# Fillers on a tile of ones at the head, weight sums over both tiles of a pair, strided probabilities turned by VectorE alone

## The chip, the cores and the metric

The kernel runs on one core of one Trainium2 chip. Its engines work side by side and meet at semaphores: TensorE (PE in the profile, its weight loads PEld), VectorE (DVE), ScalarE (ACT), GpSimd (POOL) and SyncE (SP), which here only issues transfers. The metric is the device time of one execution in microseconds, the median of several runs. In a matmul row, `ph<-xc,wi 128*128 128x512` means that the product goes to the tile ph, from a stationary 128x128 block and 512 moving columns.

## The reference, cut to what matters

Attention over 8 batches of 8 heads, 576 positions of 64 numbers, with two masks, and then a feed-forward layer on 4608 tokens:

```python
scores = scale * np.matmul(q, k.transpose(0, 1, 3, 2))
rel = pos[:, None] - pos[None, :]
mask_local = (rel >= 0) & (rel < 32)                                       # heads 0 to 3
mask_strided = (rel >= 0) & (pos[None, :] % 32 == pos[:, None] % 32)       # heads 4 to 7
attn = np.exp(scores - max); attn = attn / (sum + 1e-09)
x = np.matmul(attn, v)                  # -> [4608, 512]
h = x @ w_in                            # 512 -> 2048
g = h * np.clip(h + 3.0, 0.0, 6.0) / 6.0
return g @ w_out                        # 2048 -> 512
```

q, k and v are float32; w_in and w_out come as 64-bit floats and are turned into pairs of reduced-precision parts on the chip.

## The kernel before

**Order.** The kernel doesn't issue its work as it is written. Each piece of work (an "op") is given to a planner (class `Plan`) with the engine or engines that may do it, an estimated duration, what it reads and writes, and a due time. `Plan.emit` then plays the work through with those durations, always taking the op that can begin first (the earlier due time breaks ties), and writes one fixed order for each engine. On the chip each engine works through its list in that order and waits where a semaphore tells it to. Due times are built on the constant `T0`, the time at which the first feed-forward tile is planned to begin.

**Fillers.** Where the planner sees TensorE idle before 100 us (`WARM`), it puts fillers in: matmuls of 128x512 whose result nobody reads (function `idle`, L1625). `LIT` is the time from which TensorE can begin, `COLD` the time until which the planner counts TensorE's work 1.8 times as long and spaces fillers by `IDLE` (0.43) and not `HOT` (0.22). Before `COLD` it puts at least two fillers in front of each op. The fillers multiply `eye`, a bfloat16 identity made by GpSimd (L256 and L257), by itself. No filler is written once the second `ph` bank exists.

**The head.** Batch 0's attention comes first, in four pairs of heads. q and k are loaded in rows and turned by TensorE (L536), scores are made with the mask added by a matmul with eye (strided heads L689 and L693, local heads L659 to L670), brought to SBUF (L683 to L706), and normalized: maximum on VectorE (L724, L727), difference on GpSimd (L731, L746), exponential on ScalarE (L734, L749), sum and inverse on VectorE (L738 to L757), product on GpSimd (L742, L761). For strided heads the probabilities are then turned in blocks of 32x32 and laid on the diagonal of a cleared tile, for which the products with v (L879) need them. In batch 0 this is done in two steps: `turn` (L810), one transpose by VectorE into the kept tile `atk`, and `spread` (L817 or L819), two ops of two copies each, on ScalarE or GpSimd as the planner finds best. In later batches VectorE transposes four quarters straight into place (L807), except in batch 1, which reads `atk` as it is. In the same time the weights come in as 64-bit numbers, pass through two ScalarE steps (L340, L344), a join on VectorE (L348), a rounded high part (L356 on ScalarE, L358 on GpSimd) and a low part (L366). The first feed-forward tile (`ffn(0)`, products L1040 to L1042 and L973 to L975) begins when x and the first weights are there.

**Pairs of tiles.** Tiles 3 to 8 are done in three pairs (`PAIRS`, `ffn_pair`), with seven products in place of eight for the first layer. A pair has a first half, eight steps m of seven products into two banks `ph` (L1214 to L1216), evacuated to htmp (L1225, L1227, L1233) and gated (L1075, L1079), with the second layer of the pair's first tile in between; and a second half, 16 chunks fc of twelve products (L973 to L975) for its second tile, whose g is split into a high part (ScalarE, L1006) and a low part (GpSimd, L1009). Output weights come from DRAM into a ring of four buffers (`second_weights`, L948).

**Sums of weights.** The third pair needs sums and differences of output weights. They are made during the second pair by `combine_out(m, ...)`, once for each m from 0 to 7, out of the two weight tiles 2m and 2m+1 that are in the ring at that time: two whole sums (L1302), four differences of halves (L1306), two roundings on ScalarE (L1310), two remainders (L1313), and six stores to DRAM on SP's queue (L1318, L1321). All work in one set of four buffers, `("xf", 1, c)`, named hxf in the profile, so a sum can begin only when the stores of the sum before have been read out. The third pair loads them back (L1411).

Of the kernel before, what the change touches and what calls it, by code (L numbers as in the profile page):

```python
# [20 lines left out]
P = 128  # L21
# [8 lines left out]
PAD = 32  # L30
# [12 lines left out]

T0 = 42.0
TILE = 98.5
SOLO = 3
ADDED = 3
# [16 lines left out]
HOT = 0.22  # L66
FETCH = 2.2
BEGIN = 0.75
LIT = 1.7
LAND = 4.6  # L70
COLD = 8.6
WORDS = 256
AHEAD_OF = 63
REFILL = 3.2
# [6 lines left out]
class Plan:  # L81
# [29 lines left out]
    def emit(self, idle):  # L111
        ops = self.ops
        nexts = [[] for _ in ops]
        left = [len(o[2]) for o in ops]
        for n, o in enumerate(ops):
            for m in o[2]:
                nexts[m].append(n)
        ready = {e: [] for o in ops for e in o[0]}
        free = {e: LIT if e == "PE" else BEGIN for e in ready}
        avail = [o[9] for o in ops]  # L120
        slots = {}
        mode, dma, port = "", LAND, 0.0
        held, turned = AHEAD_OF, 0.0

        def admit(n):
            for e in ops[n][0]:
                heapq.heappush(ready[e], (ops[n][3], n))

        for n, k in enumerate(left):
            if k == 0:  # L130
                admit(n)
        order = []
        done = 0
        while done < len(ops):
            done += 1
            best = None
            for e, r in ready.items():
                t0, first, kept = free[e], None, 0.0
                for due, n in sorted(r):
                    t = max(t0, avail[n] + (PATIENCE.get((e, ops[n][11]), 0.0) if WARM < avail[n] < CALM and len(ops[n][0]) > 1 else 0.0))  # L140
                    if ops[n][11] and e in PORT:
                        t = max(t, port)
                    take = ops[n][7]
                    if take is not None:
                        many = take if isinstance(take, list) else [take]
                        s = max(kept, sorted(slots.get(k, 0.0) for k in many[0].among)[len(many) - 1])
                        if s > t and t <= t0:
                            kept = s
                        t = max(t, s)
                    if first is None or (t, due, n) < first:  # L150
                        first = (t, due, n)
                if first is not None and (best is None or first[:2] < best[3]):
                    best = (first[0], e, first[2], first[:2])
            t, e, n, _ = best
            how, fn, _, due, _, m, after, take, give, _, words, shared = ops[n]
            for x in how:
                ready[x].remove((due, n))
            for x in take if isinstance(take, list) else [take] if take else []:
                x.key = min(x.among, key=lambda k: (slots.get(k, 0.0) > t, x.among.index(k)))
                slots[x.key] = float("inf")  # L160
            if e == "PE" and t < WARM:
                one = IDLE if free[e] < COLD else HOT
                many = max(int((t - free[e]) / one), 2 if t < COLD else 0)
                t = max(t, free[e] + many * one)
                for i in range(many):
                    order.append((free[e] + i * one, len(order), None, e))
                    held += 2
            start = t
            if e == "PE" and m != mode:
                t += 0.09  # L170
                mode = m
            self.by[n] = e
            us = how[e]
            free[e] = end = t + (us() if callable(us) else us) * (1.8 if e == "PE" and t < COLD else 1.0)
            if shared and e in PORT:
                port = end - 0.13
            if e == "PE":
                held += words
                while held >= WORDS:
                    held -= WORDS  # L180
                    free[e] = end = turned = max(end, turned + (SLOWER if turned < 40.0 else REFILL))
            if after:
                end = dma = max(t + FETCH, dma) + after
            if give is not None:
                slots[give.key] = end + HOP
            order.append((start, len(order), n, e))
            for k in nexts[n]:
                hop = HOP if e not in ops[k][0] or after else 0.02
                avail[k] = max(avail[k], end + hop + ops[k][4])
                left[k] -= 1  # L190
                if left[k] == 0:
                    admit(k)
        for _, _, n, e in sorted(order):
            if n is None:
                idle()
            elif len(ops[n][0]) > 1:
                ops[n][1](e)
            else:
                ops[n][1]()
# [9 lines left out]
def attention_ffn(ctx: ExitStack, tc, q, k, v, w_in, w_out, out):  # L209
# [33 lines left out]


    three = const.tile([P, 1], F32, name="three")
    eye = const.tile([P, P], BF16, name="eye")
    mband = const.tile([QB, 2 * PAD], BF16, name="mband")
    mfirst = const.tile([PAD, PAD], BF16, name="mfirst")
# [3 lines left out]
    left = [const.tile([P, B * LEFT], F32, name=f"left{c}") for c in range(NCC)]  # L252

    def identity():
        nc.vector.memset(three, 3.0)
        make_identity(nc, new(const, ("ident",), [P, P], F32, "ident"))  # L256
        nc.gpsimd.tensor_copy(eye, tiles["ident",])  # L257
# [215 lines left out]
    def kept_pair(g):  # L473
# [318 lines left out]
        def transposes(j):  # L792
            def tr():
                e = e_whole(j)
                if apart:
                    nc.vector.transpose(tiles["atk"][:, odd, j], e)
                    return
                at = tiles[akeys[j]]
                if loc:
                    for a in range(3):  # L800
                        for h in range(2):
                            nc.vector.transpose(at[PAD * (a + h):PAD * (a + h) + PAD, :, PAD * a:PAD * a + PAD],  # L802
                                                e[PAD * a:PAD * a + PAD, :, PAD * h:PAD * h + PAD])
                else:
                    for a in range(4):
                        rows = slice(PAD * a, PAD * a + PAD)
                        nc.vector.transpose(at[rows, :, rows], e[rows])  # L807

            def turn():
                nc.vector.transpose(tiles["atk"][:, odd, j], e_whole(j))  # L810

            def spread(e, h):
                for a in (2 * h, 2 * h + 1):
                    rows = slice(PAD * a, PAD * a + PAD)
                    to, what = tiles[akeys[j]][rows, :, rows], tiles["atk"][rows, odd, j]
                    if e == "ACT":
                        nc.scalar.copy(to, what)  # L817
                    else:
                        nc.gpsimd.tensor_copy(to, what)  # L819
            if early and not loc:  # L820
                op("DVE", 0.45, turn, reads=[ekey, ekey1, wkey("o", NQ - 1, 0)], writes=[("atk", odd, j)], due=due - 2 + j)
                for h in range(2):
                    op({"ACT": 0.84, "POOL": 0.7}, 0, partial(spread, h=h), reads=[("atk", odd, j), *([akeys[j]] if h else [])], writes=[akeys[j] + ("h",)] if h else [akeys[j]], due=due - 1.9 + j)
                return
            op("DVE", 6 * 0.37 if loc else 0.45 if apart else 4 * 0.435, tr, reads=[ekey, ekey1, *home], writes=[akeys[j]], due=due - 2 + j)

        if shifted:
# [46 lines left out]
        else:  # L874
# [26 lines left out]
                op("DVE", 0.16, fence, reads=vb, writes=[stkey], due=due - 1002)  # L901
                op("PE", 0.65 * slow, partial(half_mm, 1), reads=[*akeys, *home, vkey], writes=[*vb, *xk, lk], due=due - 1001, mode="v", words=130)
            else:
                op("PE", 1.3 * slow, both_mm, reads=[*akeys, vkey, *([x + ("h",) for x in akeys] if early else [])], writes=[*vb, *xk, lk], take=vb,
                   due=due - 1001, room=0.0 if early else ROOM, mode="v", words=64)
            puts = []
            for h in range(2):
# [264 lines left out]
    def ffn_pair(p, last=None):  # L1172
# [104 lines left out]
        for m in range(HALVES):  # L1277
            if m:
                wk = [second(2 * m - 2 + i, s0 + (m + 0.3 + 0.5 * i) * long) for i in range(2)]
                if p == len(PAIRS) - 2:  # L1280
                    combine_out(m - 1, s0 + (m + 1.0) * long, wk)
            pair_products(m)
        wk = [second(NFC - 2 + i, half - (0.4 - 0.2 * i) * long) for i in range(2)]
# [2 lines left out]
        for fc in range(NFC):  # L1286
# [1 line left out]
            gk = [("g", fc % 2, x) for x in range(2)]  # L1288
            split_g(fc, kept_g[fc], gk, at - 2000, names[1])
            when = [at + 0.2 * i * short for i in range(4)]  # L1290
            mm2(fc, gk, second_weights(fc, at), when.__getitem__, names[1], None, out_of(1, half + NFC * short))

    def combine_out(m, due, wk):

# [324 lines left out]
    def idle():  # L1619

        if ("ph", 1) in tiles:
            return
        if warm[0] is None:
            warm[0] = pp.tile([P, TOK], F32, tag="ph_1", name="idle")
        nc.tensor.matmul(warm[0].rearrange("p (u x) -> p u x", x=P), eye, eye.unsqueeze(1).to_broadcast([P, TOK // P, P]), start=True, stop=True)  # L1625

    with tc.manual_schedule():
        plan.emit(idle)
# [30 lines left out]
```

## Time and profile before

| | us |
|---|---|
| median of the runs | 896.52 |
| the runs | 892.78, 896.52, 1947.74 |
| the profiled execution | 905.56 |
| its span, first to last instruction | 903.7 |
| first product of the first feed-forward tile in that span | 50.30 |
| first half of the second pair | 527 to 699 |
| its second half | 699 to 743 |

The profiled execution is the one whose rows are quoted; it is slower than the two runs of ordinary length. Views used: the page; the timeline (start, duration, engine, line, operation, the tile written and those read, and in brackets the idle time before it and what ended it); the chain of work that ended last; the waits; stretches (busy time of PE, PEld, DVE, ACT and POOL, each with its count of instructions, then granted TensorE clock, DMA share and GB/s); and groups of one line (count: shortest, median and longest ns, first and last start). "Busy" is not the same as useful: fillers are busy too.

### The profile page before, as it was taken

Reading aid. Unit: us, or ns where it says so; the run is one execution under the profiler, and the core shown is the slowest. Engines: PE = TensorE matmul, PEld = TensorE weight load, DVE = VectorE, ACT = ScalarE, POOL = GpSimd, SP = SyncE. Lnnn points to the kernel's source line nnn. Section 1 sums busy time; section 2 is a strip of 40 time slices with the busy share of each in tenths; the row PEclk is TensorE's granted clock in tenths of the full one; section 3 lists DMA queues with packets and bytes.
Section 4 is the critical chain, followed back from the end, with each engine's and each line's share of the span. In section 5 each row is a group of like instructions: output and inputs, shape, how many; then the busy total and the mean of one; then the engine's idle time right before and its main releaser. Section 6 shows DMA issues by size and latency. Waiting matters only on the chain.

```text
span 903.7 us, 20479 instructions
## 1 busy us (share of the span) xinstructions
PE 885.3 (98%) x8048; PEld 724.7 (80%) x8048; DVE 585.9 (65%) x996; ACT 401.5 (44%) x717; POOL 476.3 (53%) x429
## 2 busy tenths in 40 slices
PE   9999999999998999999999999998999999999998
PEld 6777877878887888887878878887888888888898
DVE  3778776768875767786667843657658305656882
ACT  2686664343344334434334632443456223433730
POOL 4578777357766657422232944775679732231300
PEclk9999999999999999999999999999999999999999
DMA  8978798867988899998885598899777777555632
GB/s 187 295 183 179 200 309 241 202 175 201 230 197 248 253 219 210 277 233 206 217 201 179 161 299 210 276 259 277 239 256 237 243 233 250 188 199 183 187 132 69
DMA packets 233695, 197.54 MB, mean 219 GB/s; under 512 B 164608, under 2 KB 195328, under 8 KB 233600
## 3 DMA queue, kind: packets, MB, share of 16 engines
q1 hardware_dynamic: 233444, 195.94, 77.6%
q8 instruction: 64, 1.05, 0.6%
q10 hardware_dynamic: 156, 0.29, 0.1%
q14 instruction: 31, 0.25, 0.1%
HBM read 155.29 MB, written 40.89 MB: 217 GB/s over the span
## 4 chain that ended last, share of the span: by engine, by line
PE 88%; DVE 4%; DMA 3%; ACT 2%; POOL 1%; issue 1%; SPq 0%; DVEq 0%; ACTq 0%; POOLq 0%
PE ph L1214 8%; PE ph L1215 8%; PE ph L1216 8%; PE ph L1040 5%; PE acc L973 5%; PE ph L1042 4%; PE ph L1041 4%; PE acc L975 4%; PE acc L974 4%; PE ps L670 3%; PE az L1431 3%; PE az L1429 3%; PE az L1430 3%; PE pv L879 2%; PE pv L435 2%; PE acc1b L973 2%
## 5 line engine op out<-in xcount | busy, mean ns | idle before, releaser
L1214 PE MATMUL ph<-xc,wi 128*128 128x512 f32 x336 | 134.9, 401 | 4.3 <-DVE htmp L1233 2.6
L1215 PE MATMUL ph<-xc,wi 128*128 128x512 f32 x336 | 131.8, 392 | 0.0
L1216 PE MATMUL ph<-xc,wi 128*128 128x512 f32 x336 | 131.2, 391 | 0.0
L1233 DVE TENSOR_TENSOR htmp<-ph,htmp 128x512 f32<-128x512 f32 x72 | 49.5, 689 | 57.5 <-PE ph L1216 54.3
L1009 POOL TENSOR_TENSOR g<-u,g 128x512 fp32r<-128x512 f32 x48 | 63.9, 1333 | 40.4 <-ACT g L1006 26.8
L1214 PEld LDWEIGHTS ph<-xc,wi 128*128 128x128 f32 x336 | 63.3, 188 | 21.6 <-DVE htmp L1233 3.4
L973 PE MATMUL acc<-wo,g 128*128 128x512 f32 x192 | 77.8, 405 | 0.5 <-DMA wo<-wod 0.5
L975 PE MATMUL acc<-wo,g 128*128 128x512 f32 x192 | 75.8, 395 | 2.3 <-POOL g L1009 2.3
L1040 PE MATMUL ph<-x,wi 128*128 128x512 f32 x192 | 77.2, 402 | 0.3 <-POOL wi L358 0.3
L1042 PE MATMUL ph<-x,wi 128*128 128x512 f32 x192 | 75.2, 391 | 0.6 <-POOL wi L366 0.6
L974 PE MATMUL acc<-wo,g 128*128 128x512 f32 x192 | 75.3, 392 | 0.0
L1041 PE MATMUL ph<-x,wi 128*128 128x512 f32 x192 | 75.1, 391 | 0.0
L1216 PEld LDWEIGHTS ph<-xc,wi 128*128 128x128 f32 x336 | 63.4, 189 | 13.8
L1215 PEld LDWEIGHTS ph<-xc,wi 128*128 128x128 f32 x336 | 63.4, 189 | 10.9
L802 DVE STREAM_TRANSPOSE atloc<-e 32x192 f32<-32x192 f32 x168 | 61.9, 368 | 10.0 <-POOL e L761 6.2
L1075 ACT ACTIVATE u<-ph,three 128x512 f32<-128x512 f32 x48 | 33.1, 690 | 68.0 <-PE ph L1042 67.8
L746 POOL TENSOR_TENSOR e<-e,st 128x288 f32<-128x288 f32 (+1 forms) x30 | 34.1, 1137 | 39.6 <-DVE st L724 39.4
L1225 ACT COPY htmp<-ph 128x512 f32<-128x512 f32 x58 | 34.1, 587 | 46.1 <-PE ph L1216 43.9
L761 POOL TENSOR_TENSOR e<-e,st 128x288 f32<-128x288 f32 (+1 forms) x30 | 35.4, 1181 | 33.5 <-DVE st L757 28.7
L1079 DVE SCALAR_TENSOR_TENSOR u<-u,ph 128x512 f32<-128x512 f32 x48 | 33.0, 687 | 25.3 <-ACT u L1075 24.6
L1009 POOL TENSOR_TENSOR g10a<-u,g00a 128x512 fp32r<-128x512 f32 x16 | 21.4, 1336 | 50.4 <-ACT g00a L1006 41.8
L807 DVE STREAM_TRANSPOSE at<-e 32x256 f32<-32x256 f32 x96 | 41.7, 435 | 6.1 <-POOL e L761 4.9
(318 smaller groups left out, 2330.0 us busy)
## 6 DMA issues: line engine op xcount, KB each, us to landing
wo<-wod SPq DMA_DIRECT2D x96, 512.0 KB
wi<-wid SPq DMA_DIRECT2D x84, 512.0 KB
rawi<-in_moe_w_in_dram SPq DMA_DIRECT2D x16, 512.0 KB
rawo<-in_moe_w_out_dram SPq DMA_DIRECT2D x16, 512.0 KB
wod<-wo SPq DMA_DIRECT2D x16, 512.0 KB
wid<-st SPq DMA_DIRECT2D x64, 128.0 KB
qn<-in_q_dram SPq DMA_DIRECT2D x112, 72.0 KB
kn<-in_k_dram SPq DMA_DIRECT2D x112, 72.0 KB
```

Of the source, the lines that this page charges most:

```text
L802: nc.vector.transpose(at[PAD * (a + h):PAD * (a + h) + PAD, :, PAD * a:PAD * a + PAD], e[PAD * a:PAD * a + PAD, :, PAD * h:PAD * h + PAD])
L973: nc.tensor.matmul(acc, gh, woh, start=fc == 0, stop=False)
L974: nc.tensor.matmul(acc, gh, wol, start=False, stop=False)
L975: nc.tensor.matmul(acc, gl, woh, start=False, stop=end)
L1009: on(e).tensor_tensor(out=to(1), in0=tiles[uk], in1=tiles[gk[0]].bitcast(F32), op=ALU.subtract)
L1040: nc.tensor.matmul(ph, wih, xh, start=n_ == 0, stop=False)
L1041: nc.tensor.matmul(ph, wih, xl, start=False, stop=False)
L1042: nc.tensor.matmul(ph, wil, xh, start=False, stop=n_ == NCC - 1)
L1214: nc.tensor.matmul(ph, w[:, j, 0], x[:, 0], start=u in (0, 1, 3) and j == 0, stop=False, skip_group_check=u in (2, 4, 5, 6))
L1215: nc.tensor.matmul(ph, w[:, j, 0], x[:, 1], start=False, stop=False, skip_group_check=u in (2, 4, 5, 6))
L1216: nc.tensor.matmul(ph, w[:, j, 1], x[:, 0], start=False, stop=j == 1, skip_group_check=u in (2, 4, 5, 6))
L1233: nc.vector.tensor_tensor(out=tiles[s.key], in0=tiles[bank], in1=tiles[s.key], op=ALU.add)
```

## The change

It does four things. The fillers read a new tile `full`, all ones, written by VectorE's first instruction. The planner lets fillers begin at 1.1 and puts no other TensorE work before 7.0 (`RISEN`); it counts TensorE as slow until 7.0 in place of 8.6. `T0` goes from 42 to 40. In batch 0 the strided probabilities take the path of later batches (`tr`, L807), and `turn` and `spread` go, with the extra keys that the products with v waited for. In the second pair the sums for m = 1, 3, 5, 7 stay in the first half; those for m = 0, 2, 4, 6 are made in the second half, each after the chunk fc with fc % 4 == 1, out of the ring's tiles of chunks fc-1 and fc, which the second half loads anyway.

```diff
-T0 = 42.0
+T0 = 40.0
-LIT = 1.7
+LIT = 1.1
+RISEN = 7.0
-COLD = 8.6
+COLD = 7.0
...
+            if e == "PE":
+                t = max(t, RISEN)
             if e == "PE" and t < WARM:
                 one = IDLE if free[e] < COLD else HOT
                 many = max(int((t - free[e]) / one), 2 if t < COLD else 0)
...
+    full = const.tile([P, P], BF16, name="full")
...
     def identity():
+        nc.vector.memset(full, 1.0)
         nc.vector.memset(three, 3.0)
...
-            def turn():
-                nc.vector.transpose(tiles["atk"][:, odd, j], e_whole(j))
-
-            def spread(e, h):
-                for a in (2 * h, 2 * h + 1):
...
-            if early and not loc:
-                op("DVE", 0.45, turn, reads=[ekey, ekey1, wkey("o", NQ - 1, 0)], writes=[("atk", odd, j)], due=due - 2 + j)
-                for h in range(2):
-                    op({"ACT": 0.84, "POOL": 0.7}, 0, partial(spread, h=h), ...)
-                return
             op("DVE", 6 * 0.37 if loc else 0.45 if apart else 4 * 0.435, tr, reads=[ekey, ekey1, *home], writes=[akeys[j]], due=due - 2 + j)
...
-                op("PE", 1.3 * slow, both_mm, reads=[*akeys, vkey, *([x + ("h",) for x in akeys] if early else [])], ...
+                op("PE", 1.3 * slow, both_mm, reads=[*akeys, vkey], writes=[*vb, *xk, lk], take=vb,
...
-                if p == len(PAIRS) - 2:
+                if p == len(PAIRS) - 2 and m % 2 == 0:
                     combine_out(m - 1, s0 + (m + 1.0) * long, wk)
...
-            mm2(fc, gk, second_weights(fc, at), when.__getitem__, names[1], None, out_of(1, half + NFC * short))
+            wk = second_weights(fc, at)
+            held = [wk[0]] if fc % 2 == 0 else [*held, wk[0]]
+            mm2(fc, gk, wk, when.__getitem__, names[1], None, out_of(1, half + NFC * short))
+            if p == len(PAIRS) - 2 and fc % 4 == 1:
+                combine_out(fc // 2, at + 4 * short, held)
...
-        nc.tensor.matmul(warm[0].rearrange("p (u x) -> p u x", x=P), eye, eye.unsqueeze(1)...
+        nc.tensor.matmul(warm[0].rearrange("p (u x) -> p u x", x=P), full, full.unsqueeze(1)...
```

More of the change, by code (lines that the diff above doesn't have):

```diff
@@ L807, in tr @@
                         nc.vector.transpose(at[rows, :, rows], e[rows])
-            def turn():
-                nc.vector.transpose(tiles["atk"][:, odd, j], e_whole(j))
-            def spread(e, h):
-                for a in (2 * h, 2 * h + 1):
[L814 to L819, printed above, removed]
-            if early and not loc:
-                op("DVE", 0.45, turn, reads=[ekey, ekey1, wkey("o", NQ - 1, 0)], writes=[("atk", odd, j)], due=due - 2 + j)
-                for h in range(2):
-                    op({"ACT": 0.84, "POOL": 0.7}, 0, partial(spread, h=h), reads=[("atk", odd, j), *([akeys[j]] if h else [])], writes=[akeys[j] + ("h",)] if h else [akeys[j]], due=due - 1.9 + j)
-                return
             op("DVE", 6 * 0.37 if loc else 0.45 if apart else 4 * 0.435, tr, reads=[ekey, ekey1, *home], writes=[akeys[j]], due=due - 2 + j)
@@ L903, in kept_pair @@
             else:
-                op("PE", 1.3 * slow, both_mm, reads=[*akeys, vkey, *([x + ("h",) for x in akeys] if early else [])], writes=[*vb, *xk, lk], take=vb,
+                op("PE", 1.3 * slow, both_mm, reads=[*akeys, vkey], writes=[*vb, *xk, lk], take=vb,
                    due=due - 1001, room=0.0 if early else ROOM, mode="v", words=64)
@@ L1624, in idle @@
             warm[0] = pp.tile([P, TOK], F32, tag="ph_1", name="idle")
-        nc.tensor.matmul(warm[0].rearrange("p (u x) -> p u x", x=P), eye, eye.unsqueeze(1).to_broadcast([P, TOK // P, P]), start=True, stop=True)
+        nc.tensor.matmul(warm[0].rearrange("p (u x) -> p u x", x=P), full, full.unsqueeze(1).to_broadcast([P, TOK // P, P]), start=True, stop=True)
     with tc.manual_schedule():
```

## The prediction

> **What bounds the kernel now.** I read the page first (span, busy shares, chain), then the first 54 us of the timeline, where the change does most, then the chain from 42 to 54 us, then the second pair (527 to 743 us) by waits, stretches and groups. The fences hold chosen rows; rows between them are left out.
>
> ```profile
> span 903.7 us, 20479 instructions
> PE 885.3 (98%) x8048; PEld 724.7 (80%) x8048; DVE 585.9 (65%) x996; ACT 401.5 (44%) x717; POOL 476.3 (53%) x429
> PE 88%; DVE 4%; DMA 3%; ACT 2%; POOL 1%; issue 1%; SPq 0%; DVEq 0%; ACTq 0%; POOLq 0%
> ```
>
> TensorE is busy 98% of the span and is 88% of the chain that ended last. So a gain has to shorten what TensorE does, or close its gaps. Busy is not useful, though: the head holds fillers, and useful work at half speed.
>
> ```profile
> 0.81 0.06 DVE L255 MEMSET three<- 128x1 f32 x1 [0.81 <-PEq L1643]
> 1.71 4.45 PE L1625 MATMUL idle<-eye 128*128 128x512 bf16 x10 [1.71 <-POOL eye L257]
> 6.46 1.22 PE L536 MATMUL kp<-ident,kn 72*128 72x72 f32 x8 [0.30 <-DMA kn<-in_k_dram]
> 7.48 1.06 PE L1625 MATMUL idle<-eye 128*128 128x512 bf16 x2
> 13.75 1.99 PE L693 MATMUL ps<-kplain,qt 64*128 64x72 f32 x16
> 21.14 1.52 PE L670 MATMUL ps<-kplain,qplain 64*32 64x64 f32 x72
> 31.53 3.88 PE L1625 MATMUL idle<-eye 128*128 128x512 bf16 x10
> 34.49 0.15 PEld L1625 LDWEIGHTS <-eye 128*128 128x128 bf16 x1 [0.27 <-issue]
> 34.82 0.10 PEld L1625 LDWEIGHTS <-eye 128*128 128x128 bf16 x1 [0.17 <-issue]
> 35.25 0.49 PE L659 MATMUL ps<-mband,eye 96*96 96x384 bf16 x2
> 35.83 0.97 PE L670 MATMUL ps<-kplain,qplain 64*32 64x64 f32 x72
> 41.91 5.57 PE L1625 MATMUL idle<-eye 128*128 128x512 bf16 x25
> 53.70 0.50 PE L1040 MATMUL ph<-x,wi 128*128 128x512 f32 x1
> ```
>
> The same 72 matmuls of L670 take 1.52 us at 21 us and 0.97 us at 36 us. The first ten fillers come every 4.45/10 = 0.44 us, the 25 at 41.91 every 5.57/25 = 0.22 us. Between lies the third streak of fillers: it starts at 31.53 us, and the spacing of its weight loads falls below 0.43 us at 34.8. So in this execution TensorE ran at half rate until 34.8 us. The granted clock that the page gives there is full, so in the head the spacing has to be read, not that row. The first streak (1.71 to about 6.6 us, 4.9 us long) did not lift the rate; the third did within 3.3 us. The feed-forward products run without a break only from 53.70 us.
>
> **Step 1: fillers from a tile of ones, from 1.1 to 7 us.** Now the fillers wait for eye, made by POOL (1.71 us). The new tile is one memset, first on VectorE, whose first instruction starts at 0.81 us; with 0.06 us for that one and about as much for a wider one, TensorE can start near 1.0. The diff's constants give int((7.0-1.1)/0.43) = 13 fillers; at 0.44 us they end at 1.0+5.7 = 6.7 us. The transposes of k can start at 6.46 now, so +0.2 us. The two fillers behind them (7.48, about 0.85 us on the chain) go, as the rule "at least two" holds only before 7 us: -0.85, or nothing if q lands later. I take -0.6 for both (-0.85 to +0.2).
>
> The large term is the rate. If the longer streak (5.7 us against 4.9) lifts it near 6.7 us, the work from 6.46 to 31.53, less the two fillers, 24.2 us, runs fast. L670 went to 0.97/1.52 = 0.64 of its time, fillers to 0.22/0.44 = 0.50: the gain is between 24.2x0.36 = 8.7 and 24.2x0.50 = 12.1 us. I take 8.7, since the transposes and scores here are fp32 with a weight load for each product, as in L670. Ten fillers at 31.53 would take 2.2 us in place of 3.7 (to 35.25): -1.5. Together -10.2. The low bound is -6, if VectorE, ScalarE, GpSimd and the loads, which hid behind the slow TensorE, don't follow: in 45 to 50 us TensorE waits for them already (next fence). The high one is -13.6.
>
> The Trainium skill (TensorE: Matmul & The Clock Gate, "What's actually happening") says that the rate is a clock gate that opens after a busy window of about 3.4 us, and that windows run freely, not from the kernel's start. The trace agrees: 3.3 us were enough once and 4.9 us were not. By it, as an estimate, a run of 5.7 us holds a whole window in (5.7-3.4)/3.4 = 68% of starts, one of 4.9 us in 44%. The same page's table asks only for 4 us of busy TensorE; by that the gate was open at 6 us before too, and the term of -10.2 would be nothing; the trace contradicts it.
>
> **Step 2: strided probabilities by VectorE alone.** Per head pair of this kind (two in batch 0) and per head, one transpose into a kept tile and two copies of two quarters on ScalarE or GpSimd become four transposes straight into place.
>
> ```profile
> L807 DVE STREAM_TRANSPOSE at<-e x96: 390/435/442, 177.0 to 655.5; 32x256 f32<-32x256 f32 x96
> L810 DVE STREAM_TRANSPOSE atkept<-e x4: 383/411/432, 27.1 to 43.7; 128x256 f32<-128x256 f32 x4
> L819 POOL COPY at<-atkept x8: 386/396/770, 27.6 to 48.8; 32x256 f32<-32x256 f32 x8
> 43.35 0.70 DVE L810 STREAM_TRANSPOSE atkept<-e 128x256 f32<-128x256 f32 x2
> 45.05 0.77 POOL at L819
> 45.86 0.76 POOL at L819
> 46.66 0.77 POOL at L819
> 47.50 0.83 POOL e L742
> 48.38 0.72 PE pt L835 x6
> 44.65 2.52 DVE L348 SCALAR_TENSOR_TENSOR fi<-fi,rawi 128x512 int32<-128x512 int32 x3
> ```
>
> VectorE gains 16x0.435 - 4x0.41 = 5.3 us; GpSimd loses 8 copies (at least 3.2 us), and ScalarE 8 of its own at about the same. On the chain from 42 to 50 us three of the copies (2.3 us) stand before GpSimd's second half of the normalization (47.50), for which TensorE's transposes at 48.38 wait. They go: up to -2.3. But the last eight transposes take 3.5 us from 43.35 on where two took 0.7, so the joins of the weights behind them (L348, 44.65) come up to 2.8 us later, and the first products need those: up to +2.8. I take -0.5, as GpSimd, last in that chain, also does the next step of the weights. The cover of the 25 fillers at 41.91 doesn't matter here: TensorE only waits.
>
> **Step 3: T0 from 42 to 40.** All due times built on it move 2 us ahead; it issues nothing and moves only ties in the order. Nothing, -1 to +1.
>
> **Step 4: weight sums of the second pair.**
>
> ```profile
> L1306 POOL TENSOR_TENSOR hxf<-hxf,hxf x18: 731/743/1251, 571.9 to 681.1; 128x256 f32<-128x256 f32 x18
> PE ph L1214 <- DVE htmp L1233: 2.4, 1, 2.4
> 598.09 1.29 POOL L1302 TENSOR_TENSOR hxf<-wo 128x512 f32<-128x512 f32 x1 [5.53 <-DMA wtl<-hxf]
> 613.63 1.29 POOL L1302 TENSOR_TENSOR hxf<-wo 128x512 f32<-128x512 f32 x1 [2.86 <-DMA wtr<-hxf]
> 621.05 4.42 DVE L1313 TENSOR_TENSOR hxf<-hxf,hxf 128x512 fp32r<-128x512 f32 x1 [0.34 <-POOL hxf L1306]
> 628.43 0.65 PE L1214 MATMUL ph<-xc,wi 128*128 128x512 f32 x1 [2.38 <-DVE htmp L1233]
> 632.18 0.39 PE L1214 MATMUL ph<-xc,wi 128*128 128x512 f32 x1
> 630.00:632.00 2.00, 2.00 (x6) 1.52 (x6) 1.46 (x3) 0.00 (x0) 0.95 (x1) 0.50 0.94 353
> ```
>
> The eight sums, 0 to 7, now all lie in the pair's first half (L1306: 572 to 681 us). Four (0, 2, 4, 6) move to the second half, each taking two whole sums, four halves, two roundings, two remainders, and its six stores.
>
> The one wait of TensorE in this half is here. Sum 3 started 2.86 us late, because sum 2's stores had not yet left the shared buffer hxf. Its remainder on VectorE (L1313) then took 4.42 us between GpSimd's operations, and L1233, which frees the bank, was queued behind it. TensorE lost 2.38 us, and after it nine matmuls took 632.18-628.43 = 3.75 us in place of 9x0.227 = 2.04 (0.227 us is the fast spacing, worked out below; granted clock 0.50): 4.1 us in all. With sum 2 gone, sum 3 finds its buffer free. I take -3 (-4.1 to 0: another operation may be caught like that).
>
> ```profile
> L1009 POOL TENSOR_TENSOR g11b<-g,g01b 128x512 fp32r<-128x512 f32 x10 | 12.9, 1292 | 15.0 <-ACT g01b L1006 15.0
> 720.00:730.00 10.00, 10.00 (x46) 8.29 (x45) 0.00 (x0) 2.44 (x4) 4.41 (x4) 1.00 0.61 204
> wtl<-hxf SPq DMA_DIRECT2D x16, 256.0 KB
> wtr<-hxf SPq DMA_DIRECT2D x32, 128.0 KB
> ```
>
> In the second half (about 699 to 743 us) GpSimd is free 1.5 us for each 1.29 us of L1009, VectorE is idle at 720 to 730, and the DMA engines are at 0.61 (204 GB/s). Ten microseconds there hold 46 matmuls with two cut ones, 0.227 us each, so chunks of 12 come every 2.72 us. One sum per four chunks (10.9 us) is hidden if VectorE takes its part; its stores (two of 256 and four of 128 KB) add 1 MB/10.9 us = 96 GB/s to 204, less than the 353 seen above. New waits: a load of output weights waits until a sum has read its ring slot, and behind it on SP's queue stand further loads and the stores; sums follow at 10.9 us on the one hxf, and sum 3 was late at a distance of 15. In GpSimd's queue L1009 of the next chunk stands behind a late sum. I take +1 (0 to +9.6, rival 2).
>
> **The sum.** -0.6 - 10.2 - 0.5 - 3 + 1 = -13.3. From the profiled execution's 905.56 us (span 903.7 and 1.9 around it) that gives 892.3, call it 892. Of the other runs one lies at 892.78, one at 896.52, the median. I read these as executions in which the rate rose early or nothing stalled, which no row shows; so against the median it is only -0.5%: if that run had the early rate already, only the small terms are left to gain.
>
> **Rivals.** (1) TensorE stays at half rate, or falls back. For it: 23 us of dense transposes and scores (8.3 to 31.5 us) never lifted the rate, and a wait of 2.38 us at 626 us lost it. Against: from 35 to 42 us it held, with products of the same kinds and five fillers, as the 0.22 us at 41.91 show. Time: 905.56-0.6-0.5-3+1 = 902.5. The Trainium skill (TensorE: Matmul & The Clock Gate, "Part 4: PE-mode transpose") says that transposes don't count as busy in the same way. The trace agrees as far as they didn't lift it; whether they hold it, no row shows.
>
> (2) The moved sums choke the second half; this one ends above the median of before. If GpSimd does all of a sum, it needs 2x1.29 + 4x0.74 + 2x1.29 = 8.1 us beside 4x1.29 = 5.2, that is 13.3 us per 10.9: TensorE waits 2.4 us for each of four, 9.6 in all. It decides as soon as an L1009 ends over 1.5 us late, its idle time now. Time: 892-1+9.6 = 901. Against it: VectorE's idle stretch. The Trainium skill (SBUF — State Buffer, "Who interferes with whom") says that a VectorE operation with two SBUF inputs and a GpSimd one that reads SBUF block each other; the 4.42 us of L1313 agree.
>
> (3) The change gains nothing early in the head, because VectorE, with 5.3 us more, becomes the bound there: -6 in place of -10.2 and +2.8 in place of -0.5. Time: 892+4.2+3.3 = 899.5. For it: the joins queue behind the transposes. Against it is the row below, VectorE's 0.92 us of busy time in five:
>
> ```profile
> 10.00:15.00 5.00, 5.00 (x42) 4.54 (x43) 0.92 (x2) 0.80 (x2) 0.51 (x1) 1.00 0.89 184
> ```
>
> **How the numbers follow.** Of the two streaks in the head above, one of 4.9 us failed and one of 3.3 us worked, so a longer one is likelier to work than not: forecast 0.60, rival 1 0.20, rival 2 0.12, rival 3 0.08. The forecast's own range is what its largest term leaves open: 892-3.4 = 888.6 with 13.6, 892+4.2 = 896.2 with 6. All terms at their good ends give 905.56-0.85-13.6-2.3-4.1 = 884.7. The range of 885 to 901.5 takes in rivals 2 and 3 and leaves out rival 1. 2%, about what a measurement of this kernel can tell from no change, is 878.6 to 914.5 from 896.52. No case above reaches either end; rivals 1 and 2 together give 902.5-1+9.6 = 911. So 0.02 faster, 0.96 within, 0.02 slower.
>
> **What would show it.** Step 1: the first filler near 1.0 us, 13 of them, and from the first strided scores on L693's 16 products in about 1.2 us in place of 1.99; wrong if spacing 0.43 us lasts beyond 10 us. Step 2: L807 before 50 us, no copies from atkept, L835's second batch within 3 us of the reciprocals. Step 4: no wait of TensorE near 626 us, granted clock 1.00 there, L1302 at 700 to 745 us, and no wait of L973 or L975 for L1009 or for wo. The forecast is wrong if the products without a break start later than 46 us, or if L975 waits in 700 to 745 us.

## The result, and the profile after

| | before | after |
|---|---|---|
| median of 20 runs, us | 896.45 | 893.44 |
| the runs, us | 892.47 to 903.85, and one of 1947.74 | 890.00 to 904.18 |
| ratio of the times | 1 | 0.9946 (95%: 0.9927 to 0.9964) |
| the profiled execution, us | 905.56 | 893.65 |

The change saves about half a per cent: 4.8 us by the ratio, 3.0 by the medians. That is within 2%, but the interval lies below 1. The forecast was 892.0. The ratio leaves out the run of 1947.74 us and, of after, the one of 904.18 us. Read the last line of the table with care: the two profiled executions lie 11.9 us apart, the medians 3.0 us. Besides the one of 1947.74 us, no run of before in the table took as long as 905.56 us, so the profile on which the prediction worked was of an unusually long execution. The first experiment below takes up that point.

Three lines of the page of after answer to those shown of before:

```profile
span 891.9 us, 20448 instructions
PE 871.6 (98%) x8039; PEld 713.3 (80%) x8039; DVE 618.9 (69%) x1005; ACT 401.7 (45%) x723; POOL 468.6 (53%) x411
PE 79%; DMA 6%; DVE 5%; POOL 4%; issue 2%; SPq 2%; ACT 1%; DVEq 0%; POOLq 0%; ACTq 0%
```

TensorE is busy for 13.7 us less, VectorE for 33.0 us more. TensorE's share of the chain that ended last fell from 88% to 79%, and transfers, VectorE, GpSimd and SP's queue took its place. TensorE's timeline of after (start, duration, line, operation, count, and in brackets the idle time before) shows the head:

```profile
1.05 4.80 PE L1618 MATMUL idle<-full 128*128 128x512 bf16 x13 [1.05 <-DVE full L259]
4.44 0.15 PEld L1618 LDWEIGHTS <-full 128*128 128x128 bf16 x1 [0.28 <-issue]
4.83 0.53 PEld L1618 LDWEIGHTS <-full 128*128 128x128 bf16 x3 [0.24 <-issue]
6.24 0.69 PE L541 MATMUL kp<-ident,kn 72*128 72x72 f32 x8 [0.38 <-DMA kn<-in_k_dram]
7.27 0.81 PE L1618 MATMUL idle<-full 128*128 128x512 bf16 x3
8.26 1.12 PE L698 MATMUL ps<-kplain,qt 64*128 64x72 f32 x16
15.15 0.97 PE L675 MATMUL ps<-kplain,qplain 64*32 64x64 f32 x72
31.80 0.58 PE L1029 MATMUL ph<-x,wi 128*128 128x512 f32 x1
```

Thirteen fillers start at 1.05 us. Their weight loads come every 0.4 us up to 4.83 us, and from there three fit into 0.53 us: the rate rose 3.8 us into the streak. The sixteen strided products that took 1.99 us before take 1.12, and the 72 local ones take 0.97 us already at 15 us. The first feed-forward product starts at 31.80 us; it was at 50.30 in the profile before. Now the second pair, as stretches (length; busy time of PE, PEld, DVE, ACT and POOL; granted clock; DMA share; GB/s), first of before, its first half and its second half:

```profile
527.00:699.00 172.00, 169.28 (x1211) 137.99 (x1209) 99.67 (x149) 77.50 (x133) 114.54 (x94) 0.99 0.84 255
699.00:743.00 44.00, 43.90 (x194) 36.07 (x194) 10.02 (x10) 12.28 (x20) 25.54 (x19) 1.00 0.73 238
```

In after the pair begins 15 us earlier, so its two halves are 512 to 684 and 684 to 728 us. The fence holds three more stretches of after, which are used further down:

```profile
32.00:130.00 98.00, 90.93 (x1106) 70.57 (x1104) 79.90 (x129) 63.76 (x116) 68.88 (x62) 0.97 0.89 256
200.00:300.00 100.00, 96.68 (x1047) 77.76 (x1044) 80.25 (x132) 38.29 (x73) 66.07 (x58) 1.00 0.91 233
512.00:684.00 172.00, 171.31 (x1228) 140.34 (x1227) 93.20 (x145) 74.67 (x127) 91.14 (x71) 1.00 0.78 235
684.00:728.00 44.00, 43.88 (x193) 35.76 (x193) 30.09 (x25) 17.69 (x29) 39.79 (x30) 1.00 0.83 287
600.00:640.00 40.00, 40.00 (x322) 32.82 (x321) 26.56 (x45) 18.12 (x30) 22.91 (x19) 1.00 0.78 221
```

In the second half VectorE's work went from 10.0 to 30.1 us and GpSimd's from 25.5 to 39.8, while TensorE stays at 43.9 of 44. The moved sums are hidden. In the first half TensorE gained 171.31-169.28 = 2.0 us of busy time, and its clock went from 0.99 to 1.00. The wait near 626 us is gone.

### The profile page after: what moved, and what is told of

It reads as the page before. It is cut to its first block, busy times and chain, and to the rows that moved or that the text cites. A ratio compares the mean times of both kernels' runs of the same rounds, so it can differ in the third digit from the quotient of the medians.

```text
span 891.9 us, 20448 instructions
## 1 busy us (share of the span) xinstructions
PE 871.6 (98%) x8039; PEld 713.3 (80%) x8039; DVE 618.9 (69%) x1005; ACT 401.7 (45%) x723; POOL 468.6 (53%) x411
## 3 DMA queue, kind: packets, MB, share of 16 engines
q8 instruction: 64, 1.05, 0.5%
## 4 chain that ended last, share of the span: by engine, by line
PE 79%; DMA 6%; DVE 5%; POOL 4%; issue 2%; SPq 2%; ACT 1%; DVEq 0%; POOLq 0%; ACTq 0%
PE ph L1203 8%; PE ph L1204 8%; PE ph L1205 8%; PE ph L1029 4%; PE acc L962 4%; PE ph L1031 4%; PE acc L964 4%; PE acc L963 4%; PE ph L1030 3%; PE ps L675 3%; PE az L1424 3%; PE az L1422 3%; PE az L1423 3%; DMA rawi<-in_moe_w_in_dram 2%; PE acc0b L962 2%
## 5 line engine op out<-in xcount | busy, mean ns | idle before, releaser
L1029 PE MATMUL ph<-x,wi 128*128 128x512 f32 x192 | 79.6, 414 | 2.6 <-DVE u L1068 2.3
L1031 PE MATMUL ph<-x,wi 128*128 128x512 f32 x192 | 76.1, 396 | 2.2 <-DVE wi L371 1.6
L1030 PE MATMUL ph<-x,wi 128*128 128x512 f32 x192 | 75.9, 395 | 0.2 <-DVE x L471 0.2
L1205 PEld LDWEIGHTS ph<-xc,wi 128*128 128x128 f32 x336 | 63.1, 188 | 13.7
L807 DVE STREAM_TRANSPOSE atloc<-e 32x192 f32<-32x192 f32 x168 | 61.8, 368 | 9.2 <-POOL e L766 7.1
L812 DVE STREAM_TRANSPOSE at<-e 32x256 f32<-32x256 f32 x112 | 48.7, 435 | 5.4 <-POOL e L766 4.0
L1029 PEld LDWEIGHTS ph<-x,wi 128*128 128x128 f32 x192 | 36.5, 190 | 14.1 <-DVE u L1068 5.6
```

What stands on the lines that cost most here:

```text
L1029: nc.tensor.matmul(ph, wih, xh, start=n_ == 0, stop=False)
L1030: nc.tensor.matmul(ph, wih, xl, start=False, stop=False)
L1031: nc.tensor.matmul(ph, wil, xh, start=False, stop=n_ == NCC - 1)
L1205: nc.tensor.matmul(ph, w[:, j, 1], x[:, 0], start=False, stop=j == 1, skip_group_check=u in (2, 4, 5, 6))
```

## Experiments

**Was the profile before an exception?** The kernel before was profiled again, unchanged. Beside it ran the three parts of the change one at a time.

> The kernel before, once more, for its profile. Theory A (the head's rate differs from run to run): its runs spread again from about 892 to 904, and a profile of about 896 shows the fast spacing of the matmuls early (L693's 16 products in 1.1 us, not 1.99) and the first feed-forward product near 40 us, not 50.3. Rival B (the head is always slow, and a typical run differs elsewhere): the profile shows half rate up to about 34 us at 896 as well.

It gave 896.99 us, 0.9998 (0.9970 to 1.0027) of before; its profiled execution took 896.85. The timeline, the waits, and stretches of it:

```profile
1.71 4.45 PE L1625 MATMUL idle<-eye 128*128 128x512 bf16 x10 [1.71 <-POOL eye L257]
6.58 0.72 PE L536 MATMUL kp<-ident,kn 72*128 72x72 f32 x8 [0.42 <-DMA kn<-in_k_dram]
11.29 1.11 PE L693 MATMUL ps<-kplain,qt 64*128 64x72 f32 x16
43.27 0.77 PE L1040 MATMUL ph<-x,wi 128*128 128x512 f32 x1
...
PE ph L1214 <- DVE htmp L1233: 2.8, 1, 2.8
...
32.00:130.00 98.00, 91.97 (x1127) 72.23 (x1125) 73.15 (x122) 64.00 (x118) 73.59 (x71) 0.98 0.94 254
400.00:500.00 100.00, 98.37 (x926) 79.80 (x926) 69.11 (x125) 45.47 (x80) 35.15 (x28) 0.98 0.67 193
600.00:640.00 40.00, 37.23 (x301) 30.12 (x300) 27.57 (x40) 16.50 (x28) 23.38 (x21) 0.96 0.90 260
```

In this ordinary execution the ten old fillers did lift the rate: the transposes of k take 0.72 us against 1.22, L693 1.11 against 1.99, and the first product starts at 43.27, not 50.30. So the early rate is not what the change brought. Of the 11.9 us between the profiled executions of before and after, 8.7 lie between the two profiles of the same kernel before (905.56 and 896.85), and of TensorE's 13.7 us of busy time 11.5 (e1's page has 873.8 us). Two more kernels below, e3 and e4, begin with the same ten fillers, and both have L693 in 1.11 us, e4 in an execution of 905.00 us: a long execution need not have a slow head. The wait near 626 us is here too: 2.8 us, with the clock at 0.96 in these 40 us.

**One part alone.** The fillers (`T0`, `LIT`, `RISEN`, `COLD` and the tile of ones), the sums, and the strided probabilities, each put into the kernel before:

```diff
e2:  +LIT = 1.1   +RISEN = 7.0   +COLD = 7.0   +T0 = 40.0   +nc.vector.memset(full, 1.0)
e3:  +if p == len(PAIRS) - 2 and m % 2 == 0:     +combine_out(fc // 2, at + 4 * short, held)
e4:  -if early and not loc: op(..., turn, ...); op(..., spread, ...)
```

> The kernel before with the filler part alone (the tile of ones, 1.1 to 7 us, and T0 at 40). Theory A (the early rate is the gain, most of it given back at 40 to 130 us, where VectorE and the weights bind): 1 to 2 us below before, no run above 899, first product by 35 us. Rival B (a typical run of before has the early rate already, and the sums bring all): within 0.7 us of before. Rival C (early rate is worth the full 10 us): 886.

> The kernel before with the weight sums spread, alone. Theory A: 1.5 to 2 us below before, from the wait at 626 us that goes. Rival B: 3 us below before, all of the gain. Rival D (the wait at 626 us belongs to that one profile): no difference.

> The kernel before with the strided probabilities by VectorE alone. Theory A: 0 to 1 us either way, since VectorE's 5.3 us more meet GpSimd's and ScalarE's less. Rival E (the chain through the copies is what the change gains): 2 us below before. Rival F (VectorE is the bound in the head): 1 to 3 us above before.

| part alone | median, us | ratio (95%) | first product, us |
|---|---|---|---|
| e2, fillers | 896.33 | 0.9984 (0.9955 to 1.0013) | 42.04 |
| e3, sums | 895.71 | 0.9970 (0.9947 to 0.9993) | 43.65 |
| e4, strided | 899.81 | 1.0014 (0.9986 to 1.0043) | 32.77 |

Only the sums alone are resolved as a gain, of 2.7 us. For e2 the size of Theory A fits (-1.4 us, not resolved) but not its signs: the first product isn't there by 35 us, and three runs lie above 899. It is the strided change, not the fillers, that brings the first product from 43 to 33 us, and by itself that lead brings no gain that can be measured. GpSimd's and TensorE's timelines of e1 show what held the first product back:

```profile
36.72 2.52 POOL L819 COPY at<-atkept 32x256 f32<-32x256 f32 x4
39.33 0.82 POOL L742 TENSOR_TENSOR e<-e,st 96x384 f32<-96x384 f32 x1
40.20 1.01 PE L835 MATMUL pt<-ident,e 96*128 96x96 f32 x6 [3.77 <-POOL e L742]
```

Four copies stand on GpSimd before the second half of the normalization, TensorE waits 3.77 us for that, and the first product follows at 43.27. It is the chain that the prediction read at 45 to 48 us. The stretch of 600 to 640 us, in the order e2, e3, e4, one row of each kernel's stretches:

```profile
600.00:640.00 40.00, 40.00 (x322) 32.84 (x321) 29.59 (x45) 18.46 (x31) 28.32 (x24) 1.00 0.98 291
```

```profile
600.00:640.00 40.00, 40.00 (x320) 32.47 (x319) 26.18 (x47) 18.57 (x31) 18.78 (x17) 1.00 0.76 225
```

```profile
600.00:640.00 40.00, 37.16 (x246) 29.97 (x245) 28.89 (x40) 17.52 (x29) 27.68 (x25) 0.96 0.88 269
```

The sums remove the wait, as predicted. But the fillers remove it as well, with all eight sums still in the first half. So the wait hangs on the order of the work around it, and moving the sums is not the only thing that dissolves it.

**The change without one part.**

```diff
e5:  +if early and not loc: op(..., turn, ...); op(..., spread, ...)
e6:  -if p == len(PAIRS) - 2 and m % 2 == 0:   +if p == len(PAIRS) - 2:   -combine_out(fc // 2, ...)
e7:  +skipped[0] += 1
     +if skipped[0] <= 13: return
```

> The changed kernel with the strided probabilities as before (fillers and sums changed, two-step turn kept). Theory A (the head is paced by the weights' way in, so VectorE's extra work costs nothing there): equal to the changed kernel, 0.9946 of before, within 0.002. Theory F (VectorE's 5.3 us cost time, as the 899.8 of that part alone hints): 1 to 2 us faster than the changed kernel. Theory E: 2 us slower.

> The changed kernel with all sums in the first half again. Theory A (the sums bring most of the gain): 2.5 to 4 us slower than the changed kernel, about 897, and the profile has a wait of TensorE for htmp between 600 and 640 us again. Rival G (the fillers and the order of the head bring it): within 1 us of the changed kernel.

> The changed kernel without its first 13 fillers; everything behind them keeps its order. The head then starts at half rate. Theory A (what the head loses is mostly hidden by the weights' way in, and by 130 us about half of it is left): half rate to about 20 us or beyond, first product 6 to 10 us later than 31.8, end 2 to 6 us later. Rival C (a slow head costs its full 10 us): 903. Rival H (fully hidden): within 1 us of the changed kernel.

| the change without | median, us | ratio (95%) | first product, us | dearer than the change by |
|---|---|---|---|---|
| e5, strided | 897.16 | 0.9988 (0.9966 to 1.0010) | 42.45 | 0.42% = 3.8 us |
| e6, sums | 895.96 | 0.9985 (0.9960 to 1.0009) | 32.25 | 0.39% = 3.5 us |
| e7, first 13 fillers | 900.57 | 1.0026 (1.0007 to 1.0045) | 46.16 | 0.80% = 7.2 us |

The last column is the difference of the ratios times 896.5. The interval of e7 lies far above that of the change, that of e5 just above it, and that of e6 overlaps it a little; for e5 no difference was expected. But the ratio of the change comes from other runs than these three. Beside them ran e8 (below), the change with zeros in its tile, with 0.9970 (0.9947 to 0.9994). If the zeros cost nothing, as its head suggests, e5 and e6 are dearer by 1.6 and 1.3 us only, which these intervals don't resolve, and e7 by 5.0 us, which they do. The profile of e6 shows no wait in 600 to 640 us, though all sums are in the first half: the wait that was expected there did not come back. Its row of stretches:

```profile
600.00:640.00 40.00, 40.00 (x322) 32.87 (x321) 25.67 (x43) 18.10 (x30) 27.25 (x25) 1.00 0.87 270
```

The timeline of e7, which leaves out the first thirteen fillers, is that of a head at half rate:

```profile
10.54 1.99 PE L698 MATMUL ps<-kplain,qt 64*128 64x72 f32 x16
22.28 1.52 PE L675 MATMUL ps<-kplain,qplain 64*32 64x64 f32 x72
```

These are the durations of the profile before (1.99 and 1.52). So e7 gives the price of a head that stays slow: 5 to 7 us of the end time for 14.4 us of the first product (46.16 against 31.80, where 6 to 10 us were expected). The fillers are worth that; but the kernel before had fillers too, and in the ordinary execution of e1 they did the same.

**Does the value in the tile matter?** The tile is filled with zeros in place of ones.

```diff
-nc.vector.memset(full, 1.0)
+nc.vector.memset(full, 0.0)
```

> The changed kernel with zeros in the filler tile in place of ones. If the rate answers to TensorE being busy, whatever the numbers: the rate rises at the same place (5 to 7 us) and the time is that of the changed kernel. If it answers to the numbers that pass: half rate through the head, as without the first fillers.

> The kernel with zeros in the filler tile, one look at its head. If TensorE's being busy counts: the fillers' spacing falls from 0.43 to about 0.22 us within the first streak or right behind it, and L693's counterpart (16 products) takes 1.1 us. If the numbers count: 1.99 us.

e8 gave 894.92 us, 0.9970 (0.9947 to 0.9994). Its profile is of an execution of 4810.79 us; e9 is the same kernel, in an execution of 894.73 us. The timeline of e9:

```profile
0.99 4.95 PE L1618 MATMUL idle<-full 128*128 128x512 bf16 x13 [0.99 <-DVE full L259]
8.63 1.11 PE L698 MATMUL ps<-kplain,qt 64*128 64x72 f32 x16
```

Behind zeros the rate is as high by the first strided scores as behind ones. The numbers in the tile don't decide it; TensorE's being busy is what the two have in common.

**Where does the lead in the head go?** The starts of feed-forward products, counted in the records of e1 and after (us; the products into the tiles ph and acc, 2,928 in each record):

| product | e1 (before) | after | lead |
|---|---|---|---|
| first | 43.3 | 31.8 | 11.5 |
| 86th | 67.0 | 59.3 | 7.7 |
| 146th | 87.9 | 84.1 | 3.8 |
| 301st | 130.5 | 132.3 | -1.8 |
| 2000th | 584.3 | 585.0 | -0.7 |
| end of the span | 895.0 | 891.9 | 3.1 |

The lead of 11.5 us is gone by 130 us, while the first feed-forward tiles run and the weights still come in. In these two profiles the 3.1 us at the end are gained behind the 2000th product, where e1 has its wait of 2.8 us at 600 to 640 us and after has none. Three things could pace that stretch: VectorE, which joins the weights' words and now does more transposes; the transfers; or the order in which SP issues them. Two rows of the stretches of after, between 20 and 40 us, speak for VectorE, the third busy time, at 4.76 and 4.96 us of five:

```profile
20.00:25.00 5.00, 5.00 (x105) 3.10 (x106) 4.76 (x15) 4.75 (x16) 3.53 (x6) 1.00 1.04 258
35.00:40.00 5.00, 5.00 (x110) 4.36 (x110) 4.96 (x9) 4.29 (x10) 3.71 (x4) 1.00 1.02 405
```

The chain of after in the same part (start, duration, what) speaks for the transfers and their order, that is, for the 10.94 us of a weight's load and SP's issue of batch 1's q and k (L421):

```profile
27.57 10.94 DMA rawi<-in_moe_w_in_dram
38.53 3.18 SPq L421
...
51.23 0.87 DVE fo L353
```

Each was changed by itself, on the kernel after: one more VectorE copy for each join of a weight tile; 3.1 MB of transfers more; and the last sixteen weight loads planned 16 us earlier.

```diff
e10: +nc.vector.tensor_copy(f.bitcast(F32), f.bitcast(F32))
e11: +if k >= 8: nc.sync.dma_start(more[k], src.bitcast(I32)[:, :2 * P])
e12: -... else due - 20.0, early=4.0 if k < 16 else due - 30.0
     +... else due - 36.0, early=4.0 if k < 16 else due - 46.0
```

> The changed kernel with one more VectorE copy of 128x512 behind each of the 32 joins of the weights (it copies a tile onto itself; the order of everything else stays). That is 32 x 0.4 to 0.7 = 13 to 22 us more for VectorE before 128 us. Theory I (VectorE's part of the conversion sets the pace from 35 to 130 us): 8 us or more above the changed kernel. Theory J (the loads set the pace): 3 us or less.

> The changed kernel with a quarter of each weight tile from the ninth on moved once more, from DRAM to DRAM (24 x 128 KB = 3.1 MB, 10 to 15 us at the 200 to 300 GB/s seen there). Theory J (the loads set the pace): 6 us or more above the changed kernel. Theory I (VectorE): 2 us or less.

> The changed kernel with the last 16 weight tiles' loads planned 16 us earlier, so that they stand ahead of batch 1's q and k loads on SP's queue. Theory J: 2 to 6 us faster than the changed kernel, as the head's 11 us come through. Theory I: within 2 us of it. Slower by 2 to 4 us if batch 1's attention, then late, becomes the next wait.

| | median, us | ratio (95%) | 301st product, us | last of the 32 joins ends, us |
|---|---|---|---|---|
| the change | 893.44 | 0.9946 (0.9927 to 0.9964) | 132.3 | 146.3 |
| e10, VectorE more | 900.61 | 1.0030 (1.0004 to 1.0057) | 140.4 | 156.2 |
| e11, transfers more | 893.66 | 0.9946 (0.9920 to 0.9973) | 130.2 | 144.2 |
| e12, loads earlier | 889.45 | 0.9892 (0.9846 to 0.9937) | 131.8 | 145.5 |

The groups and a stretch of e10:

```profile
L355 DVE COPY fi<-fi 128x512 f32<-128x512 f32 x13 | 11.0, 843 | 0.4
L355 DVE COPY fo<-fo 128x512 f32<-128x512 f32 x12 | 10.3, 855 | 0.4
...
32.00:130.00 98.00, 86.01 (x1086) 65.83 (x1085) 90.74 (x144) 62.11 (x113) 68.17 (x62) 0.98 0.86 237
```

In 32 to 130 us, 21.3 us of copies were added (26.8 in all), and the time rose by 0.84%, 7.5 us; the 301st product is 8.1 us later. VectorE is now at 90.7 of 98 us, and TensorE fell from 90.9 to 86.0. So VectorE's work in the head is close enough to the path that about a third of what is added to it is paid, a little less than Theory I had put. The joins fit that: their 16th ends at 79.7 us in e1 and at 70.2 in after, but the last at 147.0 and 146.3, so the lead of the joins goes as that of the products does; in e7, which is late like e10, the last ends at 155.6. More transfers cost nothing that shows.

e12 is faster than the runs of before beside it (898.47) by 9.0 us, and than the change by 4.0 us by medians (six runs; its interval and that of the change overlap from 0.9927 to 0.9937). But it doesn't show that the order of the loads matters, since its edit did less than was expected of it. Batch 1's first loads of q and k still stand ahead of the sixteen (from 37.36 us in e12, from 35.97 in after), and the last weights leave SP no earlier. SP's last issues of weights in after, then those of e12:

```profile
98.77 0.35 SPq L337 DMA_DIRECT2D rawi<-in_moe_w_in_dram  x1
99.16 2.40 SPq L337 DMA_DIRECT2D rawo<-in_moe_w_out_dram  x3
```

```profile
92.74 0.92 SPq L337 DMA_DIRECT2D rawo<-in_moe_w_out_dram  x2
101.13 0.35 SPq L337 DMA_DIRECT2D rawi<-in_moe_w_in_dram  x1
101.58 0.38 SPq L337 DMA_DIRECT2D rawo<-in_moe_w_out_dram  x1
```

TensorE is busy for 93.4 us of 32 to 130 in e12, against 90.9. Its profiled execution had a slower head than after's (first product 37.05, with a rate lost at 20 to 30 us), was at the same place at the 301st product, and led by 3.7 us at the 2000th (581.3). So in the two profiles its gain arises between 130 and 585 us, not in the head; which part of its new order brings it is not shown.

## Why the prediction was right, point by point

The time was right (892.0 forecast, 893.44 measured), and so were the signs it named, but the sum reached that time from a base that was not ordinary, and the terms do not stand for what the median gained. That the two errors, a base 9 us too high and a term of -10.2 that the median could not gain, nearly cancel is luck. The small terms alone (-0.6, -0.5, -3 and +1) give -3.1, as the medians did, but of these the runs bear out only the -3, and not its stated cause.

**Step 1, fillers: the rate right, its price and the base wrong.** The first filler at 1.05 us, thirteen of them, ending at 5.85, the transposes at 6.24: close to the forecast, which had the fillers end at 6.7. The two later fillers did not go; they became three, 0.81 us in all. The longer streak left the rate high by the first strided scores, which took 1.12/1.99 = 0.56 of their time, between the prediction's 0.50 and 0.64. Against the profile before, the first product comes 18.5 us earlier, but at the 301st product 5.4 us of that are left (137.7 against 132.3): that is nearer to the prediction's low bound of -6, with engines and loads that don't follow, than to -10.2. The term is not the median's gain either, because e1 shows that an ordinary execution of before had the rate early already. The prediction named that possibility ("if that run had the early rate already, only the small terms are left to gain"), and it is what e1 shows. What a slow head costs at the end is 5 to 7 us (e7), or at most 8.7 us (905.56-896.85, the two profiles of before, which differ elsewhere too), so -10.2 was too large even against the exception. One reading was off as well: the first ten fillers of before take 4.45 us (1.71 to 6.16) and not 4.9, which changes no term.

**Step 2, strided probabilities: the size of the effect in the head was missed, the balance was near.** Said was -0.5, between -2.3 and +2.8. Alone it measured +1.3 us (not resolved); within the change, -3.8 against the runs of the result and -1.6 against e8. The step that failed is the weighing of copies against later joins on a chain of a few microseconds: without the copies the first feed-forward product came 10 us earlier (e4: 32.77 against 43.27), of which 3.77 us are TensorE's wait behind GpSimd's copies in e1; for the rest, the order has changed: in after the first product stands ahead of the transposes (L824, 33.38 us) whose counterparts it stood behind in e1. All of it was given back by the 301st product (130.8 in e4, 130.5 in e1). VectorE does take the extra transposes, as this group of after's page shows, with 112 where there were 96, at the same 435 ns (7.0 of its 33.0 us more; the sums alone, e3, add 14.6 of busy time against e1):

```profile
L812 DVE STREAM_TRANSPOSE at<-e 32x256 f32<-32x256 f32 x112 | 48.7, 435 | 5.4 <-POOL e L766 4.0
```

**Step 3, T0:** taken as nothing; it was not tried by itself.

**Step 4, sums: the size right, the cause in part.** Forecast -3 (-4.1 to 0) for the wait near 626 us and +1 (0 to +9.6) for the second half. Moving the sums alone gained 2.7 us (0.6 to 4.8). In the profiles of e1 and after, TensorE's busy time in 600 to 640 us goes from 37.23 to 40.00 and the clock from 0.96 to 1.00. The +1 was not needed: after's second half lost 0.12 us of 44. Its ground, that the buffer shared by the sums makes the wait, is not shown: e2 and e6 lose the wait with all sums where they were, so within the change the sums may not have been needed for it.

**The rivals.** (1) Half rate was not seen in the profile of after. Its price of 902.5 us was near what e7 measured with the rate down until about 38 us, 900.57. (2) The moved sums did not choke the second half; VectorE took the part that the forecast gave it. (3) VectorE as the bound of the head was partly true: 4.76 and 4.96 us of five, and e10 shows that work added there is paid in part. Its -6 in place of -10.2 was nearer to what a slow head costs; its 899.5 is counted from the exceptional execution like the forecast, and the median came out 6 us below it.

**The sum of the parts.** The parts alone measured -1.4, -2.7 and +1.3 us (ratio less 1, times 896.5), which gives -2.8; the change as a whole measured -4.8 (-6.5 to -3.2). Each of the three intervals is 4 to 5 us wide, so they may add up or not. Each edit also gives the planner another order everywhere, and waits of 1 to 3 us come and go with it: e1 loses 1.6 us of busy time at 400 to 500 us, after loses 3.3 at 200 to 300. Which of these belong to the change and which to chance of the order stays open. Open too is where e12's gain comes from.

## What to carry to other kernels

Before a term is taken from a profile, set that execution's time beside the other runs: where it is an outlier, the largest term may be its accident, and a second profile of the same kernel settles it. A lead at the first product is no gain by itself: count later products in both traces to see where it goes, and put more work on the engine that prepares the next stage's inputs to see whether it is paid. When an experiment is faster than expected, see in its trace whether the edit moved what it was meant to move. A stall of 2 to 3 us in a planned order may vanish with any edit, so a kernel without it does not prove the cause.

## What the runs showed of the hardware

The clock row doesn't show the slow head. In e7 TensorE ran at half rate (1.99 us for L698's sixteen products) in a stretch where the granted clock is given as 1.00, as in the profile before; spacing has to be read there. The rate rose 3.8 us into the first streak of fillers in after. Behind ten fillers of 4.45 us it was up in e1 (transposes in 0.72 us) and not up in the profile before (1.22 us). The Trainium skill (TensorE: Matmul & The Clock Gate, "What's actually happening") has a window of about 3.4 us that runs freely, with which a streak of 4.45 us can do either; the runs agree.

Short waits can be enough to lose the rate. In e3 TensorE waited 1.6 us for an exponential (18.91 to 20.51 us), and then ran for ten microseconds at a clock of 0.68 and 0.63; no longer wait stands between 10 and 30 us. Not every such wait does it: behind one of 1.59 us in e9 (before 65.89 us) the clock is 1.00 for the next ten microseconds. The wait and the stretches of e3:

```profile
PE ps L689 <- ACT e L734: 1.6, 1, 1.6
...
20.00:25.00 5.00, 4.49 (x37) 3.26 (x38) 3.93 (x16) 3.46 (x8) 3.34 (x6) 0.68 0.92 248
25.00:30.00 5.00, 5.00 (x85) 2.37 (x83) 1.70 (x7) 0.84 (x2) 1.36 (x3) 0.63 1.03 241
```

The same section of the Trainium skill asks for an idle window of about 3.4 us before the rate falls; the measured wait is shorter than that, and the measurement decides. What it cost here is small: e3's first product (43.65) is as early as e1's (43.27).

The clock row missed a larger slowing too. In e8's profile the thirteen fillers took 17.17 us, 1.32 us each against 0.37 in after, while the granted clock of the whole run is given as 1.00. The row of e8's timeline:

```profile
0.99 17.17 PE L1618 MATMUL idle<-full 128*128 128x512 bf16 x13 [0.99 <-DVE full L259]
```

No run shows a cause of it.
